# A retention and adapter kernel: four batches through all their chunks, then the other four

## The chip, the core and the metric

The kernel runs on one core of a Trainium2 chip. The time is that of the device in microseconds (us); the median of three executions of the kernel before is 183.73 us (183.66 to 185.02). The engines are TensorE (PE in the profile, with its weight loads as PEld), VectorE (DVE), ScalarE (ACT), GpSimd (POOL) and SyncE (SP), which here only issues transfers. They run side by side and wait for each other by semaphores.

## What is computed

Two things one after the other. First a decayed attention without softmax, for 8 batches, 8 heads, 576 positions and 64 numbers per head, in 32-bit floats:

```python
B, H, S, D_ = q.shape                                  # 8, 8, 576, 64
scores = scale * np.matmul(q, k.transpose(0, 1, 3, 2))
gamma = 1.0 - 2.0 ** (-5.0 - np.arange(H))
rel = pos[:, None] - pos[None, :]
Dmat = np.where(rel >= 0, gamma[:, None, None] ** rel[None], 0.0)
attn = np.matmul(scores * Dmat, v)
x = attn.transpose(0, 2, 1, 3).reshape(B * S, H * D_)  # 4608 tokens x 512
```

Then for each token the two best of 8 small adapters are chosen and added:

```python
logits = x @ w_gate                                    # 512 x 8
topk = np.argpartition(-logits, 2, axis=1)[:, :2]
w = softmax of the two chosen logits
out = x + sum over the two: w * ((x @ A[e]) @ B[e])    # A[e] 512 x 16, B[e] 16 x 512
```

Because the decay is a power of the distance, a sequence can be worked chunk by chunk: a chunk needs its own queries, keys and values, and one 64x64 state per batch and head that sums up all chunks before it.

## The kernel before

**Units.** The 576 positions are four chunks of 128 (c = 0 to 3) and a short one of 64 (c = 4). The eight batches are two quads of four (`qd` = 0, 1). A full unit is two batches of one chunk. A short unit is four batches of the short chunk, two side by side in the 128 partitions. The list `units` (lines 246 to 249) goes chunk by chunk: units 0 to 3 are chunk 0 of all eight batches, 4 to 7 chunk 1, and so on to 15; units 16 and 17, called h and n, are the short chunk. Consecutive chunks of the same batches are thus four units apart.

**Steps.** Each unit goes through the same steps, which the text names by letter and unit, as U(10):

- T: TensorE transposes q and k (`pqT`, `pkT`) and ScalarE, in places VectorE, copies them to `qT` and `kT`. GpSimd then scales k in place (`scale_k`).
- S: scores (`ps`; `pe` for a short unit); VectorE multiplies them by the decay mask into `rt` (`rh`).
- Q: queries times the state `P`, into the output banks `px`. There are no matmuls in chunk 0, since there is no state yet.
- U: keys times values (`pu`). In chunk 0 VectorE multiplies this by the decay `gdec` into `P`; later VectorE adds the old state (`pn`) and GpSimd multiplies by `gdec` into `P` (line 423). Short units have no U.
- R: masked scores times values, added onto `px`; VectorE scales the result into `xT`.
- Z: logits and the first adapter product (`pz`); VectorE takes the two largest logits (`lg`, `m`, `ns`).
- V: two sigmoids on ScalarE (`sg`). W: VectorE masks and weights the adapter product (`cm`, `zc`).
- B: `xT` is transposed into `po`. X: `zc` is transposed (`pzt`), ScalarE copies it to `zT`.
- Y: the second adapter product is added onto `po`; ScalarE, in the tail also VectorE, copies it to `osb`, and SyncE stores it.

**Stages.** The loop over t (lines 671 to 765) works two full units per stage, and is called stage 4, 6 and so on after its first unit; stage 0 is written out by hand for units 0 to 3. A stage holds S of units t and t+1, in turn with T of t+2 and t+3 (from stage 8 on; earlier T stands at the end of a stage), then B, X and Y of units t-4 and t-3, in between Z of t-2 and t-1, then Q, W, U and R. After the loop comes the tail (lines 767 to 817), which works both short units through all steps and finishes units 12 to 15.

**What sets the order.** TensorE, VectorE and ScalarE get their instructions in exactly the order of the program text (`chain`, lines 73 to 87). GpSimd and SyncE are ordered by a scheduler that works at build time; on the chip every engine takes its instructions strictly in its order. A load or store whose wait has not ended holds up all those behind it on SyncE.

**PSUM banks.** The eight banks are handed out by a list (`bank` and `done`, lines 99 to 110): `bank` takes the one that has been free longest, `done` puts a bank back at the end. This happens while the program is built. On the chip the first matmul into a bank waits until the bank's last readers, named in the program before it, are through.

**Loads.** `issue(n)` (line 197) loads q, k and v of four batches of one chunk, 1 MB each, two stages before they are used. The buffers are two for q and three each for k and v. The short chunk of all batches is the ninth load, in six transfers of 64 partitions and 0.5 MB.

## Time and profile before

| | |
|---|---|
| Median of three executions | 183.73 us |
| The profiled execution | 183.08 us |
| Its span, first to last instruction | 181.4 us |
| TensorE busy | 174.4 us, 96% |
| VectorE, ScalarE, GpSimd busy | 63%, 37%, 32% |
| Read from memory, written | 28.91 MB, 9.44 MB |
| First transposes, last full matmul step | 7.50 us, 174.75 us |

All times below are from the start of the span. Busy time of TensorE includes its pipelining, so it is not TensorE at its peak; but where one step starts when the one before ends, it waits for nothing. The profile gives for each engine the busy time in 40 slices of the span, in tenths; the chain of work that ended last, followed back from the end; groups of like instructions; and a timeline of each engine. Matmuls and copies all carry the line of the helper that records them (81, 84 and 87), so they are told apart by the tiles that they write.

### The profile page before, as it was taken

The numbers are of one execution on the slowest core, as the hardware profiler recorded it, in microseconds if no ns is written. First come the engines' busy times: TensorE is split into PE (matmuls) and PEld (weight loads), VectorE is DVE, ScalarE is ACT, GpSimd is POOL, SyncE is SP. The second block draws the span as 40 slices with busy tenths as digits, with TensorE's granted clock in tenths as the row PEclk, the third lists the DMA queues.
The fourth block names the chain that finished last, engine by engine and source line by source line (L and its number), as shares of the span: only waits on it lengthen the run. The fifth ranks groups of instructions, "written<-read, shape, count | busy, mean of one in ns | idle before, by whom it ended". The sixth has DMA issues, their size and how long they took to land.

```text
span 181.4 us, 8097 instructions
## 1 busy us (share of the span) xinstructions
PE 174.4 (96%) x3606; PEld 162.7 (90%) x3606; DVE 115.1 (63%) x293; ACT 66.9 (37%) x180; POOL 58.3 (32%) x69
## 2 busy tenths in 40 slices
PE   7899999999999999999999999999999999999980
PEld 2598999999999999999999999999999999999960
DVE  4495956979566927865368717792488446558471
ACT  3603145051404252296602752075405460031461
POOL 8776108053027401687022711453050003200000
PEclk9999999999999999999999999999999999999998
DMA  6999989898898987996996999995790041014055
GB/s 147 288 253 235 304 249 274 246 318 238 244 264 246 293 266 225 277 337 210 288 311 196 254 250 356 233 207 110 246 212 12 4 184 55 4 56 184 12 225 231
DMA packets 53219, 38.74 MB, mean 214 GB/s; under 512 B 26928, under 2 KB 48576, under 8 KB 53184
## 3 DMA queue, kind: packets, MB, share of 16 engines
q1 hardware_dynamic: 50784, 37.49, 71.8%
q10 hardware_dynamic: 2224, 0.58, 1.5%
q8 instruction: 28, 0.46, 1.1%
q0 software_dynamic: 176, 0.15, 0.5%
q14 instruction: 7, 0.06, 0.1%
HBM read 28.91 MB, written 9.44 MB: 211 GB/s over the span
## 4 chain that ended last, share of the span: by engine, by line
PE 92%; DMA 3%; ACT 1%; DVE 1%; ACTq 1%; issue 0%
PE px L81 24%; PE pz L81 19%; PE ps L81 17%; PE pu L81 9%; PE po L81 9%; PE pkT L81 5%; PE pqT L81 5%; DMA k<-in_k_dram 3%; PE pzt L81 2%; PE pe L81 1%; ACT osb L87 1%; PE pa L81 1%; ACT sg L87 0%; ACTq L225 0%; DVE osb L84 0%
## 5 line engine op out<-in xcount | busy, mean ns | idle before, releaser
L84 DVE TENSOR_TENSOR rt<-ps,mask 128x512 f32<-128x512 f32 x64 | 40.3, 684 | 8.6 <-PE ps L81 7.5
L264 POOL TENSOR_TENSOR k<-k,pack 128x512 f32<-128x512 f32 x32 | 32.6, 1042 | 25.5 <-PE pkT L81 18.6
L81 PE MATMUL pz<-AW,xT 128*128 128x136 f32 x288 | 37.4, 282 | 0.0
L423 POOL TENSOR_TENSOR P<-pn,gdec 128x512 f32<-128x512 f32 x12 | 15.3, 1277 | 68.2 <-DVE pn L84 64.0
L81 PEld LDWEIGHTS pz<-AW,xT 128*128 128x128 f32 x288 | 34.7, 190 | 0.4 <-POOL AW L694 0.2
L81 PE MATMUL ps<-qT,kT 64*128 64x128 f32 x512 | 34.1, 278 | 0.1
L81 PEld LDWEIGHTS ps<-qT,kT 64*128 64x128 f32 x512 | 30.7, 188 | 1.2 <-issue 0.7
L81 PE MATMUL px<-rt,v 128*64 128x128 f32 x512 | 31.0, 273 | 0.0
L87 ACT COPY qT<-pqT 128x512 f32<-128x512 f32 (+1 forms) x33 | 16.7, 570 | 30.7 <-PE pqT L81 30.7
L81 PEld LDWEIGHTS px<-rt,v 128*64 128x64 f32 x512 | 27.9, 137 | 0.0
L84 DVE TENSOR_TENSOR xT<-px,asc 128x512 f32<-128x512 f32 x36 | 24.4, 689 | 4.1 <-PE px L81 2.8
L87 ACT COPY kT<-pkT 128x512 f32<-128x512 f32 x29 | 16.0, 601 | 26.1 <-PE pkT L81 17.3
L84 DVE COPY lg<-pz 128x16 f32<-128x16 f32 x17 | 3.0, 175 | 31.9 <-PE pz L81 31.9
L87 ACT COPY osb<-po 128x256 f32<-128x256 f32 x59 | 17.2, 387 | 2.8 <-PE po L81 2.0
L81 PE MATMUL pu<-v,k 128*64 128x64 f32 x512 | 18.1, 224 | 0.0
L81 PEld LDWEIGHTS pu<-v,k 128*64 128x64 f32 x512 | 16.6, 138 | 1.4 <-issue 1.0
L87 ACT ACTIVATE sg<-lg,ns 128x8 f32<-128x8 f32 x34 | 8.4, 294 | 24.1 <-DVE ns L84 23.7
L81 PE MATMUL px<-qT,P 64*64 64x128 f32 (+1 forms) x512 | 14.1, 259 | 0.0
L81 PE MATMUL pkT<-id,k 64*128 64x64 f32 x288 | 12.7, 224 | 0.9 <-DMA k<-in_k_dram 0.8
L84 DVE TENSOR_TENSOR pn<-pu,P 128x512 f32<-128x512 f32 x12 | 8.3, 692 | 8.3 <-PE pu L81 8.3
L81 PEld LDWEIGHTS px<-qT,P 64*64 64x64 f32 x512 | 12.5, 133 | 0.9
L81 PEld LDWEIGHTS pkT<-id,k 64*128 64x128 f32 x288 | 11.2, 139 | 2.1 <-DMA k<-in_k_dram 0.9
(59 smaller groups left out, 150.4 us busy)
## 6 DMA issues: line engine op xcount, KB each, us to landing
out_dram<-osb SPq DMA_DIRECT2D x36, 256.0 KB, 3.5
v<-in_v_dram SPq DMA_DIRECT2D x4, 512.0 KB, 6.9
q<-in_q_dram SPq DMA_DIRECT2D x3, 512.0 KB, 5.3
k<-in_k_dram SPq DMA_DIRECT2D x3, 512.0 KB, 7.5
q<-in_q_dram SPq DMA_DIRECT2D x2, 256.0 KB, 3.8
k<-in_k_dram ACTq DMA_DIRECT2D x2, 256.0 KB, 4.9
Arow<-in_moe_A_dram SPq DMA_DIRECT2D x1, 256.0 KB, 6.9
Bcat<-in_moe_B_dram POOLq DMA_DIRECT2D x1, 128.0 KB, 5.4
```

Source lines behind the costliest of these rows:

```text
L81: chain("pe", nc.tensor.matmul(*args, **kw))
L84: chain("dve", getattr(nc.vector, fn)(**kw))
L87: chain("act", getattr(nc.scalar, fn)(**kw))
L264: gp.tensor_tensor(out=kk[:, b], in0=kk[:, b], in1=gv[:, 0].unsqueeze(2).broadcast_to((128, H, Dh)), op=ALU.mult,)
L423: nc.gpsimd.tensor_tensor(out=Pt, in0=pn, in1=gdec, op=ALU.mult)
```

## The change

The order of the work is turned round. `quads` now goes through all four full chunks of batches 0 to 3 and then of batches 4 to 7, so consecutive chunks of the same batches are two units apart. Units 0 to 7 are the first quad, 8 to 15 the second, and each quad's short unit follows in the list: m = 16 for the first quad, n = 17 for the second. A short unit holds four batches of one quad instead of two from each.

Unit m is worked inside stages of the second quad: T and S in stage 8 (T before B, S after Z and V of unit 7), Q and R in stage 10 (Q ahead of Q(10), R behind Q(11)), Z, V and W in stage 12, B, X and Y in stage 14. Unit n has its T and S in stage 14 and the rest in the tail, which is rewritten. Q(2) and Q(3) now have a state to read and stand ahead of U(2); units 8 and 9 begin a sequence and have no Q matmuls. In stage 14, U(14) and U(15) stand ahead of R(14) and R(15).

The short loads are six per quad, of 64 partitions and 0.26 MB: `issue_half(0, (0, 1))` in stage 6 behind the load of quad 5 (the sixth entry of `quads`, counted from 0), v of it in stage 8, and `issue_half(1)` in stage 12. They have buffers of their own. The buffers of `qT` go from 4 to 5, `kT` from 2 to 3, `xT` from 8 to 10, `rh` from 2 to 1. Two small ScalarE copies read the last Q result of m before R(m).

In the built program, the scheduler's order on SyncE changes in stage 8: the load of k of quad 6 stood ahead of the four stores of Y(4) and Y(5) and now stands behind them.

```diff
+    NF = 2 * NQ * NFULL
...
+    def issue_half(qd, which=(0, 1, 2)):
+        key = (NFULL, qd, 0)
+        tl = nat.setdefault(key, {})
+        for i in which:
+            tag = ("qh", "kh", "vh")[i]
+            tl[i] = iop.tile([128, 2, H, Dh], FP32, tag=tag, name=tag, bufs=1)
+            for g in range(2):
+                b0 = QUAD * qd + 2 * g
+                nc.sync.dma_start(
+                    out=tl[i][64 * g : 64 * g + 64].rearrange("p s h d -> p (s h) d"),
+                    in_=(q, k, v)[i][b0 : b0 + 2, :, C * NFULL : S, :].rearrange(
+                        "s h j d -> j (s h) d"
+                    ),
+                )
...
-    quads = [(c, qd) for c in range(NFULL + 1) for qd in range(NQ)]
-    units = []
-    for c, qd in quads:
-        units += [(c, qd, 0), (c, qd, 1)] if c < NFULL else [(c, qd, 0)]
+    quads = [(c, qd) for qd in range(NQ) for c in range(NFULL)]
+    units = [(c, qd, sl) for c, qd in quads for sl in range(2)]
+    units += [(NFULL, qd, 0) for qd in range(NQ)]
...
-    for t in range(NU):
-        if units[t][2] == 0:
-            issue(quads.index(units[t][:2]) + 2, (0, 1, 2) if t <= LATE else (0,))
+    m, n = NF, NF + 1
+    for t in range(0, NF, 2):
+        issue(t // 2 + 2, (0, 1, 2) if t <= LATE else (0,))
+        if t == LATE:
+            issue_half(0, (0, 1))
+        if t == 12:
+            issue_half(1)
...
             for u in (2, 3):
+                stage_Q(u)
+            for u in (2, 3):
                 stage_U(u)
-                stage_Q(u)
                 stage_R(u)
...
+        last = t + 2 == NF
         for u in here:
             for b, nm in enumerate(("qT", "kT")):
                 stage_S(u, (b,))
-                if t > LATE:
+                if last and u == t:
+                    stage_T(n, (nm,))
+                elif t > LATE and not last:
                     stage_T(u + 2, (nm,))
...
+        if t == 8:
+            stage_T(m, shared=True)
+        if last:
+            before.append(m)
...
+        if t == 12:
+            near.append(m)
+            stage_Z(m)
+            stage_V(m)
         if t > LATE:
             issue(t // 2 + 2, (1,))
+        if t == 8:
+            stage_S(m)
+        if last:
+            stage_S(n)
+        if t == 10:
+            stage_Q(m)
+            for x in range(2):
+                act("copy", out=warm[:, x : x + 1], in_=st[m]["px"][x][:, HP - 1, L : L + 1])
         if units[t][0] > 0:
             for u in here:
                 stage_Q(u)
+        if t == 10:
+            stage_R(m)
         for u in near:
             stage_W(u)
+        if last:
+            for u in here:
+                stage_U(u)
         for u in here:
             if t > LATE and u == here[1]:
                 issue(t // 2 + 2, (2,))
-            stage_U(u)
+                if t == 8:
+                    issue_half(0, (2,))
+            if not last:
+                stage_U(u)
...
+    a, b = NF - 2, NF - 1
     stage_Q(n)
-    stage_W(h - 1)
-    stage_B(h - 2)
-    stage_B(h - 1)
-    stage_X([h - 2, h - 1])
-    stage_Z(h)
...
+    stage_B(a - 2)
+    stage_B(b - 2)
+    stage_X([a - 2, b - 2])
+    stage_Z(a)
+    stage_V(a)
+    stage_Y(a - 2, copies=("act", "dve"))
+    stage_Y(b - 2, copies=("act", "dve"))
+    stage_W(a)
+    stage_Z(b)
+    stage_V(b)
+    stage_X([a])
+    stage_W(b)
     stage_R(n)
-    stage_B(h)
-    stage_Y(h - 1, copies=("act", "dve"))
-    stage_X([h])
+    stage_B(a)
+    stage_B(b)
+    stage_Y(a, copies=("act", "dve"))
+    stage_X([b])
     stage_Z(n, (0,))
```

## The prediction

> **What bounds the kernel now.** I read the page first, for busy shares and the 40 slices, then the chain that ended last.

> ```profile
> PE 174.4 (96%) x3606; PEld 162.7 (90%) x3606; DVE 115.1 (63%) x293; ACT 66.9 (37%) x180; POOL 58.3 (32%) x69
> ...
> PE   7899999999999999999999999999999999999980
> ...
> PEclk9999999999999999999999999999999999999998
> DMA  6999989898898987996996999995790041014055
> ...
> PE 92%; DMA 3%; ACT 1%; DVE 1%; ACTq 1%; issue 0%
> ```

> TensorE is full in every slice but the first two and the last two, at full clock, and 92% of the chain is its own work. The DMA engines come second: nearly full until slice 28. So two questions decide: does the changed order make TensorE wait anywhere, and does it let a load land too late? Next, the busy times stretch by stage (columns: stretch, length, PE, PEld, DVE, ACT, POOL, clock, DMA share, GB/s); I cut at each stage's first scores.

> ```profile
> 77.57:96.92 19.35, 19.35 (x398) 18.71 (x398) 11.09 (x29) 9.64 (x25) 8.84 (x9) 1.00 0.92 286
> 96.92:116.22 19.30, 19.30 (x398) 18.66 (x398) 11.78 (x30) 8.04 (x21) 6.64 (x7) 1.00 0.86 256
> ...
> 154.81:174.75 19.94, 19.94 (x559) 18.62 (x558) 12.22 (x43) 5.99 (x20) 0.42 (x1) 1.00 0.25 94
> ```

> A stage is TensorE time from end to end, and so is the tail (third row), in which both short units lie today. There is no idle time there for the change to win back; only the last 6.65 us (174.75 to 181.40) are a chain of latencies, and the changed code ends with the same steps. The chain view prices each step (start, us, what):

> ```profile
> 99.45 0.49 PE pkT L81 x16
> ...
> 108.80 1.91 PE px L81 x64
> 110.70 1.08 PE pu L81 x32
> ...
> 161.10 1.09 PE px L81 x64
> 162.19 1.04 PE pe L81 x64
> 163.23 2.05 PE pz L81 x16
> ```

> One tensor's transposes take 0.49, Q of two full units 1.91, U 1.08, R of a short unit 1.09, S of a short unit 1.04 to 1.09, Z 1.86 to 2.05.

> **The change, part by part.** *Moved work.* Both programs issue the same matmuls, so what moves costs only what it makes wait. Q(2), Q(3) are new in stage 0 (+1.91) and Q(8), Q(9) are gone from stage 8 (-1.91), because units 8 and 9 now start a sequence. In between everything runs 1.91 later. The short unit m brings two transposes (0.99) and S (1.09) to stage 8, Q and R (1.09 each) to stage 10, Z (1.86) to stage 12, B, X and Y to stage 14. Stage 14 thus starts later by 1.91 + 0.17 + 2.18 + 1.86 = 6.12, waits not counted. From there to Z(n) today takes 172.58 - 135.52 = 37.06. Changed: four S and two transposes 4.93, three B 1.50, X 0.44, Z 1.91, three Y 1.31, Z 1.86, S(n) 1.09, Q 1.91, two U 2.01, two R 3.50, Q(n) 1.09, two B 1.14, X 0.33, Z(14) 1.91, two Y 0.87, Z(15) 1.86, X(14) 0.11, R(n) 1.09, two B 1.00, Y 0.44, X(15) 0.11: together 30.41. Net 6.12 + 30.41 - 37.06 = -0.53: the short pieces, now beside longer ones, lose some of the 0.1 to 0.2 that the tail pays at each switch. I trust this to 0.3 and take -0.3.

> *A wait at U(10).* In stage 10 the eight PSUM banks are all held: two by Z(8) and Z(9), two by Q(m), four by Q(10) and Q(11). R(m) frees two, and the free list hands its first one to U(10), which TensorE runs directly after R(m). So U(10) needs VectorE's first xT(m) done, which cannot start before R(m) ends. Its price stands among the page's groups (after the bar: busy us, mean ns of one):

> ```profile
> L84 DVE TENSOR_TENSOR xT<-px,asc 128x512 f32<-128x512 f32 x36 | 24.4, 689 | 4.1 <-PE px L81 2.8
> ```

> 0.69, plus the way there (px of unit 15 ends at 154.81, its xT starts at 154.87): 0.75 with nothing beside it. Behind U(10) in TensorE's order stand R(10), U(11) and R(11), so all of it moves. U(11)'s bank is freed by the second xT(m), hidden behind U(10) and R(10). Bounds: 0.6 to 1.4 (waiting for both).

> *A wait at X(14).* X(14) now follows Z(15), so routing of unit 14 has only Y(12), Y(13) and Z(15), 0.87 + 1.86 = 2.73, to finish. In the tail today the same steps stand in the same order on VectorE (its timeline: start, us, what; in brackets idle before):

> ```profile
> 160.26 0.17 DVE L84 COPY lg<-pz 128x16 f32<-128x16 f32 x1 [3.02 <-PE pz L81]
> ...
> 161.12 1.42 DVE L84 COPY osb<-po 128x256 f32<-128x256 f32 x4 [0.21 <-PE po L81]
> 162.45 0.35 DVE L84 SCALAR_TENSOR_TENSOR cm<-pz,m,sg 128x8 f32<-128x8 f32 x2
> 162.72 0.48 DVE L84 TENSOR_TENSOR zc<-pz,cm 128x128 f16<-128x128 f32 x2
> ```

> From Z's end (160.23) to the last zc (163.20) is 2.97. So X(14) waits 0.24, with the way 0.3. Today R(h) and S(n) lie in this gap and hide it. Next in line are xT(n) for Z(n): zc(15) ends some 2.1 after zc(14), xT(n) 0.7 later, when TensorE has R(n), two B, Y(14) and X(15), 2.75, behind it: even. Bounds 0 to 0.7.

> *The state P.* A sequence's next chunk now comes one stage after the last, not two. P is pn on VectorE, 0.69, then 1.28 on GpSimd, but Q stands half a stage further on; and before Q(n), U(14) and U(15) are put ahead of R(14), R(15), 3.50 of cover for 0.75 + 1.28 + about 0.3 of queueing. Nothing; without that cover up to 1.3. *Two tiny ScalarE copies* out of px(m) stand ahead of R(m): they end before Q(10), Q(11), 1.91, are through. Nothing. The buffer counts change no wait.

> *Loads.* SyncE issues transfers strictly in its own order. The short chunk's q and k are put behind quad 5's v, whose issue at 71.63 lands after 9.1, at 80.75. Short loads go slowly today: 197 GB/s over 116.20:125.60, against 280 over 46.00:56.50 for full ones. 1.05 MB at 197 GB/s is 5.3: k is there at 86.1. TensorE wants it at 83.52 + 1.91 + 0.50 = 85.93. A wait of 0.15 (bounds 0 to 1.5: the spread of landings).

> [...]

> In stage 8 the order of SyncE also changes: quad 6's k now stands behind the four stores of Y(4), Y(5), not ahead. SyncE's timeline today (start, us, what):

> ```profile
> 82.23 0.70 SPq L225 DMA_DIRECT2D q<-in_q_dram  x1
> 83.39 3.19 SPq L225 DMA_DIRECT2D k<-in_k_dram  x1
> 88.80 3.43 SPq L615 DMA_DIRECT2D out_dram<-osb  x4
> 92.46 0.71 SPq L225 DMA_DIRECT2D v<-in_v_dram  x1
> ```

> Y(5)'s last copy ends at 90.14 today, then 2.9 later: 93.1. The k goes out at about 93.7. Loads issued right behind stores took 6.0, 7.3, 7.4 and 8.3 to land (issues at 82.23, 65.57, 39.29 and 92.46): 99.7 to 102.0. TensorE wants it at 99.45 + 1.91 + 0.17 = 101.5. I take nothing, bounds 0 to 2.

> Sum: -0.3 + 0.75 + 0.3 + 0.15 = +0.9. The profiled execution took 183.08 (span 181.4 and 1.7 around it), so it would be 184.0; the median shown, 183.73, lies 0.65 above that execution, so I forecast 183.73 + 0.9 = **184.6 us**.

> **The rivals.** *Loads late (slower).* The same waits, and quad 6's k or the short k lands 1 to 2.5 us late, because the queue goes thin around stores. For: the 8.3 case, and DMA engines 92% busy in this stage. Against: all of stage 10's start moves with the first delay, and k's margin with it. It decides from a landing after 101.5. 183.73 + 0.9 + 1.0 to 2.5 = 185.6 to 187.1; about 186.3.

> *No new waits (not slower).* U(10) and X(14) find what they need, the short k is in time, and the fewer small pieces of the tail count between -0.3 and -0.53: 183.2 to 183.4. For: three of the four terms are under 0.5. Against: in the built program U(10) does wait for VectorE.

> *Faster by over 1%.* It would need 1.8 us of today's TensorE time to vanish; between 31.97 and 174.75 the stretches hold 0.05 idle. Only a shorter end could do it, and that is the same code.

> *The change doesn't do what it says*, say P is late everywhere because its distance is halved: 1 us in each of six stages, 190. The half stage between U and the next Q speaks against.

> **How the numbers follow.** Forecast 0.55 (with its bounds 183.9 to 185.4), loads late 0.21, no new waits 0.16, faster 0.04, P late 0.04. The range takes in the first three: 183.2 to 187.1. Within 1%, 181.9 to 185.6, is about what a measurement of this kernel cannot tell from no change; the forecast, no new waits and a tenth of loads late lie there: 0.73. Slower 0.23, faster 0.04.

> **What would show it.** Right: TensorE idle by 0.7 before pu once, in stage 10, with VectorE's xT as releaser; idle by 0.2 to 0.4 before the pzt of unit 14; stages 0, 10 and 12 longer by 1.9, 2.9 and 1.9, stage 8 by 0.2 to 0.4; from stage 14's first scores to Z(n) 30.4 to 31.0. Wrong: a pkT of stage 8 or 10 waiting for a DMA by over 0.5, px waiting for GpSimd's P, any wait in stages 2 to 6, or pieces of TensorE's own time that grow.

## The result, and the profile after

The changed kernel is slower. The median of four executions is 190.65 us (189.18 to 193.70) beside 184.34 us (183.66 to 185.02) for the kernel before, taken together with it; the ratio is 1.032 with an interval of 1.023 to 1.040. A later set of four executions of the same program gave 187.40 us (185.74 to 188.75) beside 184.00, a ratio of 1.015 (1.007 to 1.024). Both sets lie above the forecast of 184.6, and most of them above the range's end of 187.1. The medians in this document are over all executions; the ratios leave out executions more than 1.5% above the fastest of their kernel, which in some runs are those with the late loads.

The profiled execution of after took 190.62 us, with a span of 188.9. The page, as far as it answers to what was shown of before (busy shares, TensorE and its clock in 40 slices, the chain that ended last):

```profile
PE 177.3 (94%) x3606; PEld 165.8 (88%) x3606; DVE 116.2 (62%) x295; ACT 66.0 (35%) x180; POOL 58.2 (31%) x69
...
PE   7999999999999999992999999799999999999981
...
PEclk9999999999999999998589999999999999999998
...
PE 70%; SPq 16%; DMA 9%; DVE 1%; issue 1%; ACT 1%; ACTq 0%; DVEq 0%
```

The matmuls are the same 3606, but their busy time is 2.9 us longer. The slice that has a 2 is the one where TensorE waits, and the clock is down to 5 in the next one. The chain, which was 92% TensorE, now runs for 25% of the span through SyncE's issuing (SPq) and a DMA. A second, smaller dent is the 7 in slice 26.

Stage by stage (columns: stretch, length, PE, PEld, DVE, ACT, POOL, clock, DMA share, GB/s), for stages 6 and 10, and for the stretch from stage 14's first scores to Z(n):

```profile
59.68:79.00 19.32, 19.32 (x396) 18.59 (x396) 12.75 (x32) 6.78 (x20) 6.56 (x7) 1.00 0.86 244
...
105.76:128.31 22.55, 21.23 (x526) 20.65 (x526) 12.91 (x33) 8.19 (x23) 6.25 (x6) 1.00 0.87 248
...
149.46:180.30 30.84, 30.84 (x696) 29.36 (x696) 18.87 (x56) 10.23 (x32) 2.92 (x3) 1.00 0.24 88
```

Stage 6 is TensorE from end to end as before, and so is the stretch from stage 14 to Z(n). Stage 10 lacks 1.32 us of TensorE. Set against the first scores of the same stages in before, and against the prediction's own terms:

| From, to | Before | After | Change | Predicted |
|---|---|---|---|---|
| start to stage 8 | 77.57 | 79.00 | +1.43 | +1.91 |
| stage 8 | 19.35 | 26.76 | **+7.41** | +0.32 |
| stage 10 | 19.30 | 22.55 | +3.25 | +2.93 |
| stage 12 | 19.30 | 21.15 | +1.85 | +1.86 |
| stage 14 to Z(n) | 37.06 | 30.84 | -6.22 | -6.35 |
| Z(n) to the end | 8.82 | 8.60 | -0.22 | 0 |
| span | 181.4 | 188.9 | +7.5 | +0.67 |

The predicted column has the -0.53 that the prediction worked out (it then took -0.3). All of the miss stands in stage 8. TensorE's timeline there (start, us, what; in brackets the idle time before and what ended it):

```profile
87.64 0.24 PE L81 MATMUL pqT<-id,qh 64*128 64x64 f32 x1 [2.64 <-DMA qh<-in_q_dram]
...
90.10 1.08 PE L81 MATMUL pkT<-id,kh 64*128 64x64 f32 x15 [0.57 <-DMA kh<-in_k_dram]
90.90 1.99 PE L81 MATMUL po<-id,xT 64*128 64x64 f32 x32
...
93.22 3.21 PE L81 MATMUL pz<-AW,xT 128*128 128x136 f32 x16
```

The chain in front of it goes through SyncE's issues, of quad 5's v (L207) and of the short q and k (L236), to the landing of the short k:

```profile
75.17 3.36 SPq L207
...
84.86 5.11 DMA kh<-in_k_dram
```

T(m), the transposes of the short chunk, would have run from 85.0 to 85.98. It waits for q and again for k, and its last part starts 4.6 late, at 90.10. After the wait each step is too long: the 15 transposes take 1.08 where 16 took 0.49, the pz of Z(6) 3.21 here and 2.07 in before. The clock shows why (same columns as the stages):

```profile
87.00:88.00 1.00, 0.24 (x1) 0.14 (x1) 0.00 (x0) 0.00 (x0) 0.07 (x1) 1.00 0.32 67
...
94.00:95.00 1.00, 1.00 (x6) 1.00 (x6) 0.00 (x0) 0.05 (x1) 0.00 (x0) 0.50 1.05 283
...
96.00:97.00 1.00, 1.00 (x11) 0.91 (x10) 0.47 (x4) 0.00 (x0) 0.00 (x0) 1.00 0.30 87
```

From 88.70 to 95.53, 6.83 us, the granted clock is 0.50. On the chain B(4) and B(5) take 1.71 instead of 1.00, `pzt` 0.54 instead of 0.33, `pz` 3.00 instead of 1.91: 2.0, and with the transposes 2.6. So stage 8 is 0.17 of moved work, 4.6 of delay by the loads (3.65 of it with TensorE idle) and 2.6 of half clock: 7.4.

### The profile page after: what moved, and what is told of

Read it like the earlier page. It is cut to its first block, busy times and chain, and to the rows that moved or that the text cites. A ratio compares the mean times of both kernels' runs of the same rounds, so it can differ in the third digit from the quotient of the medians.

```text
span 188.9 us, 8103 instructions
## 1 busy us (share of the span) xinstructions
PE 177.3 (94%) x3606; PEld 165.8 (88%) x3606; DVE 116.2 (62%) x295; ACT 66.0 (35%) x180; POOL 58.2 (31%) x69
## 4 chain that ended last, share of the span: by engine, by line
PE 70%; SPq 16%; DMA 9%; DVE 1%; issue 1%; ACT 1%; ACTq 0%; DVEq 0%
PE px L81 18%; PE pz L81 16%; PE ps L81 12%; SPq L207 11%; PE po L81 8%; PE pu L81 6%; DMA k<-in_k_dram 6%; PE pkT L81 4%; SPq L236 3%; DMA kh<-in_k_dram 3%; PE pqT L81 3%; SPq L171 2%; PE pzt L81 2%; PE pe L81 1%; DVE xT L84 0%
## 5 line engine op out<-in xcount | busy, mean ns | idle before, releaser
L84 DVE TENSOR_TENSOR rt<-ps,mask 128x512 f32<-128x512 f32 x64 | 40.2, 683 | 8.6 <-PE ps L81 8.1
L81 PE MATMUL pz<-AW,xT 128*128 128x136 f32 x288 | 37.9, 287 | 0.0
L81 PEld LDWEIGHTS pz<-AW,xT 128*128 128x128 f32 x288 | 35.7, 195 | 0.1
L81 PE MATMUL ps<-qT,kT 64*128 64x128 f32 x512 | 33.5, 278 | 0.2 <-DVE kT L84 0.2
L81 PEld LDWEIGHTS ps<-qT,kT 64*128 64x128 f32 x512 | 30.5, 188 | 1.2 <-issue 0.3
L81 PE MATMUL px<-rt,v 128*64 128x128 f32 x512 | 30.8, 273 | 0.0
L84 DVE TENSOR_TENSOR xT<-px,asc 128x512 f32<-128x512 f32 x36 | 24.3, 688 | 7.3 <-PE px L81 6.4
L81 PEld LDWEIGHTS px<-rt,v 128*64 128x64 f32 x512 | 28.0, 137 | 0.0
L87 ACT COPY kT<-pkT 128x512 f32<-128x512 f32 x28 | 15.5, 600 | 29.1 <-PE pkT L81 28.6
L84 DVE COPY lg<-pz 128x16 f32<-128x16 f32 x17 | 3.0, 174 | 33.7 <-PE pz L81 33.7
L81 PE MATMUL pu<-v,k 128*64 128x64 f32 x512 | 17.9, 224 | 1.3 <-DVE xT L84 1.3
L81 PEld LDWEIGHTS pu<-v,k 128*64 128x64 f32 x512 | 16.5, 138 | 2.6 <-issue 2.1
L81 PE MATMUL px<-qT,P 64*64 64x128 f32 (+1 forms) x512 | 13.9, 259 | 0.0
L87 ACT COPY zT<-pzt 128x512 f16<-128x512 f16 (+3 forms) x12 | 5.8, 480 | 21.1 <-PE pzt L81 21.1
L81 PEld LDWEIGHTS px<-qT,P 64*64 64x64 f32 x512 | 12.4, 133 | 0.8 <-issue 0.2
L81 PE MATMUL pkT<-id,k 64*128 64x64 f32 x256 | 11.4, 227 | 0.6 <-DMA k<-in_k_dram 0.6
L81 PEld LDWEIGHTS pkT<-id,k 64*128 64x128 f32 x256 | 10.0, 142 | 1.6 <-issue 0.8
```

Of the source, the lines that this page charges most:

```text
L81: chain("pe", nc.tensor.matmul(*args, **kw))
L84: chain("dve", getattr(nc.vector, fn)(**kw))
L87: chain("act", getattr(nc.scalar, fn)(**kw))
```

## The experiments

The runs follow the order in which the questions came up. In the edits, lines are those of the changed kernel.

**Is the wait for the short chunk the whole loss?** T(m) is given data that is there already.

```diff
+            nat[units[m]][0] = nat[units[m]][1] = nat[units[10]][0]
```

> The changed kernel, with one thing taken away: T(m) reads q of quad 5, which has long landed, in place of the short chunk's q and k, so the first four batches' short chunk is not computed; the short loads are still issued. Theory A (the short load lands about 5 us after TensorE is ready for it, and the idle time then halves TensorE's clock for the next 6.8 us, another 2.0): 190.65 - 5.2 - 2.0 = 183.4 us, within 1% of the kernel before. Rival B (the loss lies in the new waits at U(10) and X(14) and in the new order of the work, and the landing only shifts it): 187 us or more.

Measured: 188.05 us (185.65 to 190.06), ratio 1.012 (1.009 to 1.015). Two of the four executions took about 186 us and two 190; even the faster two miss theory A's 183.4, and rival B's number comes out for a reason that it doesn't give. The profiled execution is one of the slower two (190.06, span 188.3). It has no wait at T(m). It waits one stage later, at quad 6's k. TensorE's timeline:

```profile
105.20 1.11 PE L81 MATMUL pkT<-id,k 64*128 64x64 f32 x16 [3.95 <-DMA k<-in_k_dram]
```

and SyncE's (issues):

```profile
91.42 6.85 SPq L612 DMA_DIRECT2D out_dram<-osb  x4
98.90 0.74 SPq L207 DMA_DIRECT2D k<-in_k_dram  x1
```

The four stores of Y(4) and Y(5) stand ahead of that k. Their last copy ended at 92.77, close to the 93.1 of the prediction, but the issues held the queue until 98.27, and k went out at 98.90, not at 93.7. It landed at 105.06, 6.2 later, as the prediction's rows said. TensorE had run out of work at 101.25 (predicted 101.5), and the clock was 0.50 from 103.53 for 6.83 us. So there are two late loads, one behind the other, and the first had been hiding the second: in after everything is later by the first wait, quad 6's k goes out at 101.02 and lands at 107.29, and TensorE, which wants it at 108.12, doesn't wait for it at all.

**What does the clock cost?** A first attempt: twelve matmuls that nobody reads, put ahead of T(m), so that TensorE doesn't rest.

```diff
+            filler = bank([128, 512], "filler")
+            for _ in range(12):
+                mm(filler, lhsT=idle[:, 0:128], rhs=idle, start=True, stop=True)
+            done(filler)
```

> The changed kernel with 12 dummy matmuls on a buffer of zeros ahead of T(m), about 2.6 us at full clock, so that TensorE is busy for half of its wait. Theory A with the clock driven by TensorE's idleness: the wait stays but the granted clock stays at 1.00 behind it, 190.65 - 2.0 = 188.6 us. Rival (the clock drop has another cause, or costs nothing since everything waits for transfers anyway): 190.6 us and a clock of 0.50 in the windows behind T(m).

Measured: 188.54 us (187.48 to 190.97), ratio 1.025 (1.020 to 1.030). In the profiled execution (187.48) the loads happened to be early (quad 5's v at 80.74, the short k at 85.68), so there was no wait to fill and the filler was plain work; that the median meets theory A's 188.6 shows nothing. The order on SyncE had changed too: quad 6's k stood ahead of the stores and landed at 97.79. It decides nothing on the clock's price; the last pair of runs takes that up.

**Do the loads run slower because of the addresses that they now read?** The full loads of after are sent to the places that before reads at the same turn, and the other way round.

```diff
+        sc, sq = (n // 2, n % 2)
...
-                    QUAD * qd + lo : QUAD * qd + hi, :, C * c : C * c + C, :
+                    QUAD * sq + lo : QUAD * sq + hi, :, C * sc : C * sc + C, :
```

> The changed kernel with every full load reading the addresses that the kernel before reads at that place in the sequence of loads (so the output belongs to mixed-up chunks); sizes, order and buffers are unchanged. Theory C (going along one quad's chunks makes the stream of loads some 4 us slower by quad 5): v of quad 5 lands near 81 us in place of 84.7, T(m) waits about 1 us, no half clock, 184 to 185 us. Rival D (the stream's pace differs from execution to execution, not by addresses): landing 83 to 85, 189 to 191 us.

> The kernel before with every full load reading the addresses that the changed kernel reads at that place (mixed-up chunks in the output). Theory C: v of quad 5 lands near 84.7 us in place of 80.75; the kernel before has margins of 3.7 us and more from stage 8 on and some 1 to 3 us before, so its time stays within 1% of 184.3. Rival D: landing as in the kernel before.

Measured: after with the old addresses 186.69 us (185.88 to 188.67), ratio 1.015 (1.010 to 1.021); before with the new ones 184.48 us (183.45 to 187.53, ten executions), ratio 1.002 (0.998 to 1.006). Changing the addresses moves neither kernel by what these runs can tell: the first ratio is that of the changed kernel's second set, 1.015. Quad 5's v landed at 82.12 and at 83.23. Neither landing is what theory C or rival D asked for, and the unchanged program's second profile, below, has 82.22. The addresses aren't shown to be the cause.

**The same kernel again, and each load moved.** The runs of this part ran on one chip and share their comparisons, but for the one with only quad 6's k moved. First after, unchanged:

> The changed kernel itself once more, beside the others on the same chip. If the pace of the loads differs from execution to execution, v of quad 5 lands anywhere from 80.7 to 84.7 us in its profile and the time follows it: 186 us with the early landing, 190.6 with the late one.

Measured: 187.40 us (185.74 to 188.75). The profiled execution is the fastest one, 185.74, span 184.0. TensorE's timeline in stage 8:

```profile
87.64 0.68 PE L81 MATMUL pkT<-id,kh 64*128 64x64 f32 x15 [1.44 <-DMA kh<-in_k_dram]
```

The short k landed at 87.51 instead of 89.96, the only wait for it is 1.44, the clock doesn't fall there (0.996 over the span), and quad 6's k (102.74) is in time. 1.4 here, 1.3 at U(10) and 0.2 at X(14) make 2.9; the span is 2.6 over that of before, so -0.3 is left for the moved work. So two executions of one program differ by 4.9 us, and what differs is the landing of the loads: quad 5's v at 84.66 in the first profile, at 82.22 in this one.

Now the short q and k go out ahead of quad 5's v, which is wanted later:

```diff
-        issue(t // 2 + 2, (0, 1, 2) if t <= LATE else (0,))
         if t == LATE:
+            issue(t // 2 + 2, (0, 1))
             issue_half(0, (0, 1))
+            issue(t // 2 + 2, (2,))
+        else:
+            issue(t // 2 + 2, (0, 1, 2) if t < LATE else (0,))
```

> The changed kernel with the short chunk's q and k put ahead of quad 5's v instead of behind it (v is not wanted before stage 10). Theory A1 (two late loads: the short k, and behind it quad 6's k, which stands behind stores): the short k now lands near 82 to 85.5, T(m) waits 0.5 us or less, but quad 6's k still lands at 100 to 105 where TensorE wants it at 101.5, so the time is 184.5 to 187 us, with a wait of pkT for quad 6's k in the slower of them. Rival (the short load alone is the loss, quad 6's k was late in the run without the landing only because everything there was earlier): 184.3 us or less in every execution and no such wait.

Measured: 187.60 us (184.92 to 191.68), ratio 1.010 (1.000 to 1.021). The short k is there at 83.52 and T(m) doesn't wait; quad 6's k lands at 104.14 behind the stores, and TensorE waits 3.0 for it and then runs at half clock for 3.41 us:

```profile
104.27 1.12 PE L81 MATMUL pkT<-id,k 64*128 64x64 f32 x16 [2.97 <-DMA k<-in_k_dram]
```

This is the first experiment's result, with the whole computation kept.

Only quad 6's k moved, ahead of the stores:

```diff
-        issue(t // 2 + 2, (0, 1, 2) if t <= LATE else (0,))
+        issue(t // 2 + 2, (0, 1, 2) if t <= LATE else (0, 1) if t == 8 else (0,))
...
-        if t > LATE:
+        if t > 8:
             issue(t // 2 + 2, (1,))
```

> The changed kernel with quad 6's k alone issued at the start of stage 8, ahead of the stores; the short q and k stay behind quad 5's v. Theory A1: the wait at T(m) is left and differs with the pace of the loads (1.4 us with v of quad 5 landing at 82.2, 5 us and a halved clock with 84.7), so 185.5 to 190 us, and no wait for quad 6's k. Rival (quad 6's k is the larger half): 184 to 185 us, as with both loads moved.

Measured (on another chip): 187.29 us (183.81 to 189.65, ten executions), ratio 1.006 (1.000 to 1.012). The profiled execution (189.65) waits 1.5 for the short q and 1.3 for the short k and has the half clock too, with a mean of 0.979 over the span as in after. The fall shows in the steps: a single transpose takes 0.34 at 88.12, where one took 0.24 at 84.76, and the 15 of k take 1.08 at 88.90, where the 15 of q took 0.68:

```profile
84.76 0.24 PE L81 MATMUL pqT<-id,qh 64*128 64x64 f32 x1
86.55 0.68 PE L81 MATMUL pqT<-id,qh 64*128 64x64 f32 x15 [1.55 <-DMA qh<-in_q_dram]
88.12 0.34 PE L81 MATMUL pkT<-id,kh 64*128 64x64 f32 x1 [0.89 <-DMA kh<-in_k_dram]
88.90 1.08 PE L81 MATMUL pkT<-id,kh 64*128 64x64 f32 x15 [0.45 <-DMA kh<-in_k_dram]
```

Of the ten, the six whose mean clock was under 0.99 took 186.6 to 189.65, the four others 183.81 to 187.31.

Both moved, with the two edits together:

> As the last one, and quad 6's k issued at the start of stage 8, right behind its q, so that it stands ahead of the stores on SyncE. Theory A1: quad 6's k lands near 98, TensorE waits for no transfer from stage 8 on and its clock stays at 1.00 to the end: 184.0 to 184.8 us (the waits at U(10), 1.3, and X(14), 0.5, are left, less 0.5 to 0.9 of shorter steps). Rival B (the order itself costs): 186 us or more.

Measured: 184.56 us (183.65 to 185.03), ratio 1.002 (0.996 to 1.009), span of the profiled execution 181.9. No load is waited for from stage 8 on (the short k lands at 84.04, quad 6's k at 99.46), and the clock is 0.999. All that TensorE waits for in this execution by more than 0.15 us at a time:

```profile
PE pu L81 <- issue: 1.3, 1, 1.3
PE spare L81 <- DVE warm L152: 1.3, 1, 1.3
PE pqT L81 <- DMA q<-in_q_dram: 0.8, 1, 0.8
PE pkT L81 <- DMA k<-in_k_dram: 0.6, 2, 0.4
PE pzt L81 <- DVE zc L84: 0.5, 1, 0.5
```

The first is the wait at U(10); the others lie ahead of 15 us or in the last 6 us. Either move alone keeps one of the two waits; together they bring the time back to that of before.

**The wait at U(10).** In after, on the chain that ended last (start, us, what):

```profile
117.64 3.84 PE px L81 x192
...
121.48 0.41 issue
121.89 0.70 DVE xT L84
...
122.73 1.15 PE pu L81 x32
```

R(m) ends at 121.48, xT(m) starts 0.41 later and takes 0.70, and U(10) starts 1.25 after R(m). To take the wait away, W of units 8 and 9 is named ahead of R(m) in the program, so that it gives back the banks of Z(8) and Z(9) first and U(10) gets one of those. TensorE's own order stays as it was.

```diff
-        if t == 10:
-            stage_R(m)
         for u in near:
             stage_W(u)
+        if t == 10:
+            stage_R(m)
```

with both loads moved as in the run before:

> As the last one, and W(8), W(9) put ahead of R(m) in the program, so that the bank list hands U(10) a bank of Z(8), long read, in place of R(m)'s. Theory: the wait before U(10), 1.3 us, is gone: 1.3 less than the last one, 182.7 to 183.5 us, level with the kernel before or just under. Rival (the wait only moves on, to S(12), whose banks are then those of R(m) or wait for W's work on VectorE, which is done later): no difference.

> The version with both loads moved and W before R(m) once more, in more rounds: 182.7 to 184.4 us, between 0.5% under and level with the kernel before. Rival: it keeps a slow execution now and then, since its loads still run with margins of 2 to 5 us, so its spread is wider than that of the kernel before.

Measured: 183.96 us (183.16 to 190.34), ratio 0.998 (0.991 to 1.006), and on the second chip, with twelve executions, 184.78 us (182.32 to 186.38), ratio 0.997 (0.992 to 1.002). The chain of the first:

```profile
110.70 3.77 PE px L81 x192
114.47 1.08 PE pu L81 x32
...
116.32 0.41 issue
```

U(10) starts at once, so the bank was the reason for its wait. But 0.41 of waiting shows up inside R(10), and stage 10 is 21.89 long instead of the 22.51 with only the loads moved: 0.6 is won of the 1.3 expected, and the rival, that the wait moves on, is half right. This version is level with before: the intervals hold 1, and no gain is shown. More of its executions are long, though, as the second expectation's rival had it in part: one of 190.34 on the first chip, and six of the twelve on the second over 185 us, where 5 of before's 23 were (one of them 188.76); over all executions the median there is 0.8 above before's 183.98.

**The price of the clock by itself.** In the last version, a wait of fixed length is put ahead of T(m): a matmul, nine ScalarE copies one after the other, and a matmul that reads the last. In one kernel TensorE rests meanwhile, in the other it runs 22 matmuls that nobody reads (the diff shows the resting one; the busy one has 22 in the place of the 0).

```diff
+    scr16 = padp.tile([128, 128], FP16, tag="scr16", name="scr16")
...
+            gate, other = [bank([128, 512], f"gate{x}") for x in range(2)]
+            flat = pick.rearrange("p a b -> p (a b)")
+            mm(gate, lhsT=idle[:, 0:128], rhs=idle, start=True, stop=True)
+            act("copy", out=flat, in_=gate)
+            for _ in range(7):
+                act("copy", out=flat, in_=flat)
+            act("copy", out=scr16, in_=flat[:, 0:128])
+            for _ in range(0):
+                mm(other, lhsT=idle[:, 0:128], rhs=idle, start=True, stop=True)
+            mm(other, lhsT=scr16, rhs=idle, start=True, stop=True)
+            done(gate, other)
```

> That version with a wait made on purpose ahead of T(m): TensorE waits for a chain of nine ScalarE copies, some 5 to 6 us, whatever the transfers do, and is idle meanwhile. Theory (an idle TensorE has its clock halved for some 6.8 us): the granted clock is 0.50 behind the wait, and the kernel takes about 2 us more than the one with the busy wait, some 191 to 192 us. Rival (the half clock in the changed kernel's run belonged to something else): as the busy wait.

> The same chain of ScalarE copies and the same wait, but TensorE runs 22 dummy matmuls, some 4.7 us, while it lasts. Theory: the granted clock stays at 1.00, and the time is that of the version without a wait plus the chain, 5 to 6 us: 188.5 to 190 us.

Measured: resting 192.47 us (191.72 to 192.69), ratio 1.045 (1.039 to 1.050); busy 190.82 us (189.83 to 191.65), ratio 1.036 (1.030 to 1.042). TensorE's timeline, resting:

```profile
92.66 0.61 PE L81 MATMUL gate<-idle,scr 128*128 128x512 f16 x1 [6.22 <-ACT scr L87]
...
94.96 1.90 PE L81 MATMUL po<-id,xT 64*128 64x64 f32 x32
```

and busy:

```profile
93.42 0.39 PE L81 MATMUL gate<-idle,scr 128*128 128x512 f16 x1 [1.48 <-ACT scr L87]
...
94.80 1.16 PE L81 MATMUL po<-id,xT 64*128 64x64 f32 x32
```

The same steps after the same chain of copies take 1.90 or 1.16 (B), with the clock at 0.50 from 89.90 to 96.73 or at 1.00 (0.999 over the span). From the matmul that ends the wait to S(m) it is 9.11 us resting (92.66 to 101.77) and 7.43 busy (93.42 to 100.85), 1.68 more; the medians differ by 1.65, and the ranges don't overlap. That is what the half clock costs here beside the wait itself: 2.76 of its 6.83 us fell into the rest, so 4.07 us were slowed. Both medians lie about 0.5 to 0.8 above what was expected; the chain of copies took 6.6 us from matmul to matmul in both kernels, not 5 to 6. In after, where more work lay in the 6.83 us, the half clock cost 2.6.

## Why the prediction was wrong

**The step that failed is the one on loads**, in both of its places: the waits were foreseen, and their size was wrong. "1.05 MB at 197 GB/s is 5.3" was right: from quad 5's v to the short k were 5.30 us in after, 5.29 in its second profile. But the 5.3 was put onto the 80.75 of one execution. In the eight traces with after's order, or before's, up to that v, it landed at 80.74, 80.75, 82.12, 82.22, 83.23, 83.71, 84.66 and 84.68; the prediction had stood on the early end, with "the spread of landings" set to 1.5. The wait called 0.15 was 4.6 and 1.4 in the two profiles of after. The second place, quad 6's k, was given as "nothing, bounds 0 to 2", from an issue at 93.7. With T(m)'s wait out of the way it was 95.96 to 98.90, because the four stores ahead of it held the queue for 3.85 to 6.85 us, where they took 3.43 in before, and TensorE waited 3.0 to 3.95. Before's own trace had a warning: another four of its stores held the queue for twice as long.

```profile
74.94 7.07 SPq L615 DMA_DIRECT2D out_dram<-osb  x4
```

**What was missing is the clock.** No term had it, because before's trace has no idle time of TensorE in the middle. The last pair shows it, with 1.65 us, and the profile of after has 2.6 of it, more than the whole rise that was forecast. In the resting kernel TensorE was idle from 86.44 and had the half clock from 89.90, 3.46 later. In after itself the longest gap before the fall was 2.64, and with only quad 6's k moved it was 1.55.

**The rival "loads late" had the right place**, both loads by name, and the wrong price: 1 to 2.5 in all. Its reason, a queue that goes thin around stores, isn't what made the short k late: that came 5.3 after quad 5's v, as worked out, and v was late. Quad 6's k was issued late, and landed 6.2 and 8.2 after its issue (without T(m)'s wait), inside the prediction's rows of 6.0 to 8.3. The argument against the rival, that k's margin moves with the first delay, holds too: in after the first wait hid the second. But it hides it by being paid.

**The other terms stood.** *Moved work*: stages 0, 12 and 14 went nearly as worked out (+1.79 from S(2) to stage 4's first scores, +1.85 and -6.22). Span less waits and clock leaves 7.5 - 4.6 - 2.6 - 1.3 - 0.2 = -1.2 in the first profile of after and -0.3 in the second; with both loads moved it is -0.9. The -0.3 that was taken is one end of these, so that the second profile meets it is partly luck. In the first, 0.5 of it lies ahead of stage 8. *U(10)*: the wait is there, once, in stage 10, on xT(m); it is 1.3 instead of 0.75, inside the bounds of 0.6 to 1.4, by the 0.4 that VectorE started late. The waits of TensorE in after (what waited for what: us in total, times, longest):

```profile
PE pqT L81 <- DMA qh<-in_q_dram: 3.1, 2, 2.6
PE pu L81 <- DVE xT L84: 1.3, 1, 1.3
```

*X(14)*: on the chain of after its two transposes take longer than the two of X(15) behind them:

```profile
176.98 0.43 PE pzt L81 x2
...
180.19 0.11 PE pzt L81 x2
```

The second one starts at 177.2, after the last zc (ends 177.12): 0.2 to 0.3 of waiting, where 0.3 was predicted. *P and the ScalarE copies*: no px waits for P anywhere in after, and stages 4 and 6 have no wait; stage 0 waits 0.6 in all for full loads of k, where before waits 0.8. One figure of the working is slightly off by its own prices and changes nothing: the 2.75 behind xT(n) adds to 2.64. *No gain*: right; with the loads moved and W put first, the new order is level with the old.

What stays open: why the loads run at a different pace from one execution to the next, why the four first executions of after were slower than the later four (one of each four was profiled), and why xT(m) starts 0.4 late. The addresses were tried and aren't shown to matter; the others weren't tried.

## What to carry to other kernels

A load whose margin is near zero in one trace is late in others: take the landing from several executions, here over a range of 4 us, and price the late end too. A late load on TensorE's path costs its wait and, where the clock falls as well, the half clock: another 2.6 us in after, 1.65 in the resting kernel against the busy one. In the profiles here the clock fell in stages with a longest wait of 1.55 us and more, and not in those with one of 1.44 (second profile of after) and 1.48 (busy kernel). And mending the first late load only uncovers the next, so look at all of them, and at what the scheduler has put ahead of them on the queue, before one is moved.

## What the runs showed of the hardware that was not expected

The clock fell without one long gap. In the run with only quad 6's k moved TensorE's gaps up to the fall were 1.55 and 0.89 us, and the fall lies between 87.23, where 15 transposes have ended at full pace (0.68), and the single one of 88.12 (0.34 instead of 0.24). In the changed kernel the longest gap before the fall at 88.70 was 2.64; in the first experiment the fall came 2.3 us into the gap. The second profile of after, with one gap of 1.44 us in stage 8, has no such fall (0.996 over the span), nor has the busy kernel with one of 1.48 (0.999). The half clock lasted 3.41 us where work followed without a gap (short q and k moved), but 6.83 us in after, the first experiment and the resting kernel, where TensorE still had some idle time behind the fall.

SyncE's issue of four stores took 1.9 to 7.1 us for the same 1 MB (1.93 in after, 6.85 in the first experiment, 7.07 in before), and the loads behind them waited that long to be issued.
